# Words of weights fetched a block ahead, and quotients on another engine, in a kernel of hash attention and an MLP mixer

## The chip, the cores and the metric

The kernel runs on one core of a Trainium2 chip. A core has five engines with an instruction queue each, and each works through its queue in order: TensorE (PE in the profile, with its weight loads shown apart as PEld) multiplies matrices, VectorE (DVE) and ScalarE (ACT) work element by element, GpSimd (POOL) does so too, and SyncE (SP) issues transfers. SBUF is the memory in which tiles lie; PSUM holds what TensorE sums up. Engines wait for each other by semaphores. The metric is the device time of one execution in microseconds (us), as the median of several runs; less is better.

## The reference

Two blocks, one behind the other. `q`, `k`, `v` have the shape 4 x 8 x 768 x 64 (batch, head, position, feature).

```python
q_bits = (np.einsum('bhsd,dk->bhsk', q, proj) > 0)        # 6 bits, k likewise
mask = q_bucket[:, :, :, None] == k_bucket[:, :, None, :]  # the same 6 bits
scores = scale * np.matmul(q, k.transpose(0, 1, 3, 2))
scores = np.where(mask, scores, -1000000000.0)
attn = np.exp(scores - np.max(scores, axis=-1, keepdims=True))
attn = attn / (np.sum(attn, axis=-1, keepdims=True) + 1e-09)
x = np.matmul(attn, v)            # heads side by side: 4 x 768 x 512
...
xt = x.transpose(0, 2, 1)
h = np.maximum(xt @ w_tok1, 0.0) @ w_tok2        # over positions
u = x + h.transpose(0, 2, 1)
h2 = np.maximum(u @ w_ch1, 0.0) @ w_ch2          # over channels
return u + h2
```

The four matrices of weights come as 64-bit floats. The kernel reads each as two 32-bit words and rounds it to 32 bits itself.

## The kernel before

It has three stages.

**Attention** (`attention`). The 32 heads are worked on in 16 pairs, a pair in two halves of 384 queries. `Half.scores` multiplies keys by queries for the six groups of 128 keys (L299), each with a second product of hash bits (`bits`) that lowers the scores of other buckets; `exponential` on ScalarE (L306) makes the tiles `e`, of which there are twelve, two halves' worth. `Half.add` adds the six tiles `e` of a half up: GpSimd adds two of them (`esa`, L329), VectorE the others (L331, L332, L334) and then the two sums (L335). `Half.weigh` multiplies `e` by the values `vn` (L345, result `acc`), and ScalarE moves the result to `num` with a bias `vsum` (L351). `Half.weigh` of a half is queued behind the scores of the next half.

Once the two halves of a pair are done, `Quotients` follows in the first half of the next pair: TensorE sums over partitions (`sums`, L369), ScalarE makes a first value of the reciprocal (`near`, L373 and L374), VectorE improves it (`newton`, L382 to L390), and `divide` multiplies `num` by it into `XT` (L394, GpSimd). In the same first half `hashes` makes the bits of the next pair: TensorE (`hp`, L266), VectorE (`g`, L271 and L274), and eight small transfers on SyncE that put them into `bits` (L280). Three tiles of `bits` take turns. `load_qk` and `load_v` fetch queries, keys and values of later pairs; `add_values` (ScalarE, L257) adds the transposed values `vt` up into `vsum`.

**Conversion.** Beside this, `Conversion` rounds the weights in blocks of 128 x 768. A block has three thirds, one in each half from the second pair on, 30 halves in all: `begin` (ScalarE L165, VectorE L167 and L170), `join` (VectorE L182, GpSimd L185 and L186) and `end` (ScalarE L195, VectorE L196). `some` runs them in turn, between the half's additions and its `weigh`. The words of a block lie in the tile `raw`, of which attention has one, and `fetch` (L154, SyncE) asks for the next block's words after `end`. Attention converts eight blocks (`w_tok1`, `w_tok2` and half of `w_ch1`) in 24 of the halves.

**Tokens** (`tokens`). `turn` transposes a batch on TensorE (L226) and ScalarE copies it (L227); `mix1` (L570) and `mix2` (L583) are the two products over positions, and VectorE adds the result to `XT` (L589). A list of jobs, one after each step, rounds the twelve blocks left, with three buffers of `raw`, and forms sums of weights (`weight_sums`, L613 to L618). `inputs` (L540 to L544) forms sums of `XT`.

**Channels** (`channels`). The two products over channels, with 7 block products in place of 8 (L639), and the outputs. Beside them VectorE looks at all queries and keys for their largest value (`look`, `decide`); from it comes a flag `unsafe`. At the very end all engines read the flag (L835) and branch: when it is set, the whole is computed again in a safer way, which these inputs don't ask for.

The order on each engine is the order in which the code calls its operations; nothing rearranges it.

Of the kernel before, what the change touches and what calls it, by code (L numbers as in the profile page):

```python
# [48 lines left out]
def kernel(  # L49
# [13 lines left out]
    nc = tc.nc  # L63
# [62 lines left out]
    class Conversion:  # L126
# [30 lines left out]
        def begin(self):  # L157
            if not self.fetched:
                return
            raw, to, rows = self.fetched.pop(0)  # L160
            lo, hi = raw[:, :, 0], raw[:, :, 1]
            tmp = self.pool.tile([P, 2, NW], F32, name="tmp", tag="cvt", bufs=min(self.bufs, 2))
            big = tmp[:, 0].bitcast(U32)

            nc.scalar.activation(lo.bitcast(F32), lo, ACT.Copy, scale=2.0**-52)  # L165

            nc.vector.tensor_scalar(  # L167
                big, hi, 3, 0x3FFFFFFF, op0=ALU.logical_shift_left, op1=ALU.bitwise_and,
            )
            nc.vector.scalar_tensor_tensor(  # L170
                big, hi, 0xC0000000, big, op0=ALU.bitwise_and, op1=ALU.bitwise_or,
            )
            self.begun = raw, tmp, to, rows
# [27 lines left out]
        def some(self, k):  # L201

            (self.begin, self.join, self.end)[k]()
            if k == 2:
                self.fetch()

        def one(self):
# [20 lines left out]


    def attention(pool, psum, W1, W2, x0):  # L230
        zeroed = [pool.tile([P, 2, S], BF16, name=f"bits{n}", tag=f"bits{n}", bufs=1) for n in range(3)]
        loaded = {}

        def load_qk(n):
# [8 lines left out]
        def load_v(n):  # L243
            if n >= len(pairs):
                return
            b, hp = pairs[n]
            vn = pool.tile([P, 2, NR, D], F32, name="vn", tag="vn", bufs=3)
            nc.sync.dma_start(out=vn, in_=v[b, hp])
            vt = pool.tile([P, S], F32, name="vt", tag="vt", bufs=2)
            nc.sync.dma_start(out=vt, in_=vT[b, hp])  # L250
            loaded[n][1:3] = vn, vt

        def add_values(n):

            vt = loaded[n][2]
            vsum = pool.tile([P, 1], F32, name="vsum", tag="vsum", bufs=4)
            nc.scalar.activation(vt, vt, ACT.Copy, scale=-EPS, accum_out=vsum)  # L257
            loaded[n][3] = vsum

        def hashes(n):  # L260

            g = pool.tile([P, HALF], BF16, name="g", tag="g", bufs=2)
            ps = psum.tile([P, 2, 512], F32, name="hp", tag="sc", bufs=3)[:, 0]
            for j in range(4):
                sl = slice(HALF * (j // 2), HALF * (j // 2) + HALF)
                nc.tensor.matmul(  # L266
                    ps[32 * j : 32 * j + 32, :HALF], projblk, loaded[n][0][:, j % 2, sl],
                    start=True, stop=True,
                )
            for rows in [slice(0, 64), slice(64, P)] if n == 0 else [slice(0, P)]:  # L270
                nc.vector.tensor_scalar(  # L271
                    g[rows], ps[rows, :HALF], 0.0, 0.5, op0=ALU.is_gt, op1=ALU.subtract,
                )
                nc.vector.tensor_scalar(g[rows], g[rows], bitscale[rows], None, op0=ALU.mult)  # L274
            for j in range(4):
                sl = slice(HALF * (j // 2), HALF * (j // 2) + HALF)
                for i in range(2):
                    at = 32 * j + 16 * i
                    issuer = nc.scalar if n == 0 and i else nc.sync
                    issuer.dma_start(  # L280
                        out=zeroed[n % 3][D * i : D * i + NB + 1, j % 2, sl], in_=g[at : at + NB + 1],
                    )

        class Half:
# [4 lines left out]

            def scores(self):  # L290

                qkt, bits = loaded[self.n][0], zeroed[self.n % 3]
                qs = slice(HALF * self.half, HALF * self.half + HALF)
                first = self.n == self.half == 0

                def product(sc, t, c, start):
                    for i in range(2):
                        rows = slice(D * i, D * i + D)
                        nc.tensor.matmul(  # L299
                            sc[:, i, :HALF], t[rows, 1, P * c : P * c + P], t[rows, 0, qs],  # L300
                            start=start, stop=not start,
                        )

                def exponential(sc):
                    e = pool.tile([P, 2, HALF], F32, name="e", tag="e", bufs=12)
                    nc.scalar.activation(e, sc[:, :, :HALF], ACT.Exp, scale=SCALE)  # L306
                    self.es.append(e)

                waiting = []
                for c in range(NR):  # L310
                    sc = psum.tile([P, 2, 512], F32, name="sc", tag="sc", bufs=3)
                    product(sc, qkt, c, True)
                    if first and c < GR:
                        waiting.append((c, sc))
                        if c == GR - 1:
                            for c, sc in waiting:
                                product(sc, bits, c, False)
                            for c, sc in waiting:
                                exponential(sc)
                        continue  # L320
                    product(sc, bits, c, False)
                    exponential(sc)
# [34 lines left out]
        class Quotients:  # L357
# [33 lines left out]

            def divide(self):
                b, hp = pairs[self.n]
                nc.gpsimd.tensor_tensor(  # L394
                    XT[:, hp, S * b : S * b + S].rearrange("p (h q) -> p h q", h=2),
                    nums.pop(self.n), self.rec, op=ALU.mult,
                )
# [9 lines left out]
        for _ in range(14):  # L407
            nc.tensor.matmul(idle[:D, :D], ones, ones, start=True, stop=True)
        hashes(0)
        load_v(0)  # L410
        load_v(1)
        weights = Conversion(
            pool,
            [(w_tok1, W1, 3, (0, NR)), (w_tok2, W2, 1, (0, NJ)), (w_ch1, WC1, 1, (0, NCB // 2))],
            bufs=1,
        )
        before, both = None, []
        third = 0
        for n in range(len(pairs)):
            for half in range(2):  # L420
                now = Half(n, half)
                now.scores()
                if n == half == 0:
                    add_values(0)
                now.add(0)
                quotients = None
                if len(both) == 2:
                    quotients, both = Quotients(both), []
                    quotients.sums()
                both.append(now)  # L430
                if half == 0 and n + 1 < len(pairs):
                    hashes(n + 1)
                    load_qk(n + 2)
                if half == 1 and n + 1 < len(pairs):
                    add_values(n + 1)
                if quotients:
                    quotients.newton()
                now.add(1)
                if n:
                    weights.some(third)  # L440
                    third = (third + 1) % 3
                if before:
                    before.weigh()
                if quotients:
                    quotients.divide()
                if half == 0:
                    load_v(n + 2)
                before = now
        while third or weights.fetched:
            weights.some(third)  # L450
# [171 lines left out]
    def channels(pool, psum, SW1, WC2, SW2, T, judge):  # L622
# [135 lines left out]
        for s in range(last + 1):  # L758
            rs = []
            for t in range(HC):  # L760
                r = pool.tile([P, 4, TT], F32, name="r2", tag="r2", bufs=HC)
                hidden(s, t, r)
                rs.append(r)
                if s or t:
                    look()
                if judge and s == last and t == 1:
                    assert not unseen
                    rest = decide()
                if judge and s == last and t == 4:
                    rest()  # L770
            outputs(s, rs)

    def inside(stage, *args):
# [15 lines left out]
    def attention_and_tokens(W1, W2, x0):  # L789
# [6 lines left out]

        def weights(pool):
            return Conversion(
                pool, [(w_ch1, WC1, 1, (NCB // 2, NCB)), (w_ch2, WC2, 3, (0, NHT))], bufs=3,
            )  # L800

        def jobs(conversion):
            n1, n2 = (NCB // 2) * DCH // NW, NHT * DM // NW
            return [
                *[conversion.one] * (n1 + 1),
                *weight_sums(
# [24 lines left out]
        inside(tokens, W1, W2, x0, None, None, [big["T"][0], None, big["T"][1], None])  # L831

    with_token_weights(attention_and_tokens)
    inside(channels, big["SW1"], big["WC2"], big["SW2"], big["T"], True)
    flag = nc.values_load(unsafe, min_val=0, max_val=1)  # L835
    with tc.If(flag > 0):
        with_token_weights(careful_attention_and_tokens)
        inside(channels, big["SW1"], big["WC2"], big["SW2"], big["T"], False)

# [41 lines left out]
```

## Time and profile before

| | |
|---|---|
| median of 3 runs | 887.88 us (887.83 to 888.03) |
| the profiled execution | 890.64 us |
| its span, first to last instruction | 888.7 us |
| its mean granted TensorE clock | 0.987 |

Busy time of the engines by stage, in the profiled execution (us from the start of the span):

| stage | TensorE | VectorE | ScalarE | GpSimd |
|---|---|---|---|---|
| attention, 0 to 345 | 325.86 | 262.42 | 211.04 | 145.00 |
| tokens, 345 to 450 | 99.79 | 83.24 | 38.37 | 55.84 |
| channels, 450 to 888.7 | 433.05 | 198.01 | 56.17 | 48.73 |

A row of a timeline reads: start and duration in us, engine, line, operation, what it writes and reads, the shape, how many in one, and in brackets how long the engine was idle before it and what ended that. A row of a line's own view gives the shortest, the median and the longest duration in ns and the first and last start. In the chain of work that ended last, a row has start, duration and what the end waited for.

### The profile page before, as it was taken

Reading aid. Unit: us, or ns where it says so; the run is one execution under the profiler, and the core shown is the slowest. Engines: PE = TensorE matmul, PEld = TensorE weight load, DVE = VectorE, ACT = ScalarE, POOL = GpSimd, SP = SyncE. Lnnn points to the kernel's source line nnn. Section 1 sums busy time; section 2 is a strip of 40 time slices with the busy share of each in tenths; the row PEclk is TensorE's granted clock in tenths of the full one; section 3 lists DMA queues with packets and bytes.
Section 4 is the critical chain, followed back from the end, with each engine's and each line's share of the span. In section 5 each row is a group of like instructions: output and inputs, shape, how many; then the busy total and the mean of one; then the engine's idle time right before and its main releaser. Section 6 shows DMA issues by size and latency. Waiting matters only on the chain.

```text
span 888.7 us, 9246 instructions
## 1 busy us (share of the span) xinstructions
PE 858.7 (97%) x3545; PEld 398.6 (45%) x3545; DVE 543.7 (61%) x625; ACT 305.6 (34%) x445; POOL 249.6 (28%) x140
## 2 busy tenths in 40 slices
PE   8998998998999999999899999999999999999997
PEld 4443443443444445455444444444444444444444
DVE  2686986896886777598984475434448342336411
ACT  3765666656656664334312110002120101211000
POOL 3352552553454422556621111201111200111110
PEclk8999999999999999999999999999999999999999
DMA  5223323323332201233211211131220120000001
GB/s 181 98 74 104 117 87 116 131 76 110 109 104 80 73 3 52 92 107 106 71 36 36 72 35 60 35 142 36 71 72 0 60 83 24 1 0 1 24 24 52
DMA packets 20644, 61.16 MB, mean 69 GB/s; under 512 B 2800, under 2 KB 4464, under 8 KB 20592
## 3 DMA queue, kind: packets, MB, share of 16 engines
q1 hardware_dynamic: 20536, 60.46, 20.0%
q8 instruction: 30, 0.49, 0.2%
q14 instruction: 22, 0.18, 0.1%
q10 hardware_dynamic: 56, 0.02, 0.0%
HBM read 53.49 MB, written 6.29 MB: 67 GB/s over the span
## 4 chain that ended last, share of the span: by engine, by line
PE 81%; DVE 10%; DMA 3%; ACT 2%; issue 2%; POOL 1%; SPq 0%; DVEq 0%; ACTq 0%
PE b L639 49%; PE sc L299 13%; PE acc L345 10%; PE t L570 4%; PE t L583 3%; DMA raw<-in_moe_w_tok 2%; DVE esd L335 2%; ACT e L306 1%; PE sums L369 1%; DVE WC L196 1%; DMA raw<-in_moe_w_ch 1%; DVE tmp L170 1%; PE hp L266 1%; PE trp L226 1%; DVE rec L390 1%
## 5 line engine op out<-in xcount | busy, mean ns | idle before, releaser
L299 PE MATMUL sc<-qk 64*128 64x384 f32 x768 | 166.9, 514 | 15.9 <-ACT e L306 15.5
L306 ACT ACTIVATE e<-sc 128x768 f32<-128x768 f32 x192 | 151.5, 811 | 29.8 <-PE sc L299 29.7
L646 ACT COPY p<-b 128x512 f32<-128x512 f32 x72 | 42.1, 585 | 294.2 <-PE b L639 294.2
L345 PE MATMUL acc<-e,vn 128*64 128x384 f32 x768 | 130.9, 490 | 0.0
L639 PE MATMUL b<-r,WC 128*128 128x512 f32 (+1 forms) x300 | 125.6, 575 | 0.0
L299 PEld LDWEIGHTS sc<-qk 64*128 64x128 f32 x768 | 69.4, 195 | 75.9 <-issue 44.9
L639 PE MATMUL b<-T,SW 128*128 128x512 f32 x216 | 96.6, 592 | 0.0
L665 POOL TENSOR_TENSOR p<-p,p 128x512 f32<-128x512 f32 x18 | 22.9, 1271 | 238.9 <-ACT p L646 238.9
L329 POOL TENSOR_TENSOR esa<-e 128x768 f32<-128x768 f32 x32 | 71.0, 2224 | 67.3 <-ACT e L306 67.3
L639 PEld LDWEIGHTS b<-r,WC 128*128 128x128 f32 x300 | 57.0, 190 | 67.1 <-issue 64.1
L345 PEld LDWEIGHTS acc<-e,vn 128*64 128x64 f32 x768 | 52.3, 137 | 74.9 <-issue 74.2
L185 POOL TENSOR_TENSOR tmp<-tmp,raw 128x768 f32<-128x768 f32 x20 | 41.6, 2082 | 100.4 <-DVE tmp L182 63.0
L639 PE MATMUL b<-T,WC 128*128 128x512 f32 x144 | 67.7, 592 | 0.0
L331 DVE TENSOR_TENSOR esd<-e 128x768 f32<-128x768 f32 x32 | 37.1, 1159 | 49.1 <-ACT e L306 49.1
L299 PE MATMUL sc<-bits 64*128 64x384 bf16 x384 | 64.9, 332 | 1.3 <-DMA bits<-g 1.3
L669 DVE TENSOR_TENSOR r<-p,u 128x512 f32<-128x512 f32 x18 | 12.4, 691 | 86.7 <-ACT u L646 86.7
L639 PE MATMUL b<-XT,WC 128*128 128x512 f32 x144 | 64.7, 592 | 0.0
L639 PEld LDWEIGHTS b<-T,SW 128*128 128x128 f32 x216 | 41.0, 190 | 51.7 <-issue 49.7
L639 PE MATMUL b<-r,SW 128*128 128x512 f32 x144 | 62.8, 592 | 0.0
L394 POOL TENSOR_TENSOR XT<-num,rec 128x768 f32<-128x768 f32 x16 | 37.5, 2346 | 77.1 <-ACT num L351 39.7
L335 DVE SCALAR_TENSOR_TENSOR esd<-esd,esa 128x768 f32<-128x768 f32 x32 | 52.8, 1649 | 9.7 <-POOL esa L329 6.8
L186 POOL TENSOR_TENSOR tmp<-tmp 128x768 f32<-128x768 f32 x20 | 46.0, 2302 | 1.6
(84 smaller groups left out, 952.2 us busy)
## 6 DMA issues: line engine op xcount, KB each, us to landing
raw<-in_moe_w_ch SPq DMA_DIRECT2D x16, 768.0 KB
seen<-in_qk SPq DMA_DIRECT2D x16, 768.0 KB
qk<-in_qk SPq DMA_DIRECT2D x15, 768.0 KB
vn<-in_v SPq DMA_DIRECT2D x16, 384.0 KB
vt<-in_vT SPq DMA_DIRECT2D x16, 384.0 KB
out<-p SPq DMA_DIRECT2D x18, 256.0 KB
raw<-in_moe_w_tok SPq DMA_DIRECT2D x4, 768.0 KB
bits<-g SPq DMA_DIRECT2D x124, 5.2 KB
```

The source lines that it names most:

```text
L185: nc.gpsimd.tensor_tensor(unit, unit, lo, op=ALU.mult)
L186: nc.gpsimd.tensor_tensor(big, big, unit, op=ALU.add)
L299: nc.tensor.matmul(sc[:, i, :HALF], t[rows, 1, P * c : P * c + P], t[rows, 0, qs], start=start, stop=not start,)
L306: nc.scalar.activation(e, sc[:, :, :HALF], ACT.Exp, scale=SCALE)
L329: nc.gpsimd.tensor_tensor(self.a, es[0], es[1], op=ALU.add)
L331: nc.vector.tensor_tensor(self.d, es[2], es[3], op=ALU.add)
L335: nc.vector.scalar_tensor_tensor(self.d, self.d, NR * EPS, self.a, op0=ALU.add, op1=ALU.add,)
L345: nc.tensor.matmul(acc[D * i : D * i + D], vn[:, i, c], e[:, i], start=(c == 0), stop=(c == NR - 1),)
L394: nc.gpsimd.tensor_tensor(XT[:, hp, S * b : S * b + S].rearrange("p (h q) -> p h q", h=2), nums.pop(self.n), self.rec, op=ALU.mult,)
L570: nc.tensor.matmul(ps, W1[:, r, P * j : P * j + P], x[:, r], start=(r == 0), stop=(r == NR - 1),)
L639: nc.tensor.matmul(self.ps[i][:, cols], left(k), right(k)[:, cols], start=first and k == ks[0], stop=k == ks[-1], skip_group_check=True,)
L646: nc.scalar.copy(c, self.ps[i])
```

## The change

Five edits go together.

- In attention `raw` gets a second buffer, and `fetch` follows `begin` in place of `end`, so a block's words are asked for when the block before begins.
- `divide` runs on VectorE.
- Attention converts two more blocks (three of the four rows of `w_ch1`, ten blocks, 30 halves); the tokens stage has two fewer, and two jobs fewer.
- For room in SBUF there are two tiles of `bits` and of `vn` in place of three; values are loaded one pair ahead in place of two, and `add_values` of a pair runs in its own first half, not in the second half of the pair before.
- The flag is read ahead of the last `outputs`.

```diff
-            tmp = self.pool.tile([P, 2, NW], F32, name="tmp", tag="cvt", bufs=min(self.bufs, 2))
+            tmp = self.pool.tile([P, 2, NW], F32, name="tmp", tag="cvt", bufs=self.bufs - 1)
...
             (self.begin, self.join, self.end)[k]()
-            if k == 2:
+            if k == 0:
                 self.fetch()
...
-        zeroed = [pool.tile([P, 2, S], BF16, name=f"bits{n}", tag=f"bits{n}", bufs=1) for n in range(3)]
+        zeroed = [pool.tile([P, 2, S], BF16, name=f"bits{n}", tag=f"bits{n}", bufs=1) for n in range(2)]
...
-            vn = pool.tile([P, 2, NR, D], F32, name="vn", tag="vn", bufs=3)
+            vn = pool.tile([P, 2, NR, D], F32, name="vn", tag="vn", bufs=2)
...
                 b, hp = pairs[self.n]
-                nc.gpsimd.tensor_tensor(
+                nc.vector.tensor_tensor(
                     XT[:, hp, S * b : S * b + S].rearrange("p (h q) -> p h q", h=2),
...
         load_v(0)
-        load_v(1)
         weights = Conversion(
             pool,
-            [(w_tok1, W1, 3, (0, NR)), (w_tok2, W2, 1, (0, NJ)), (w_ch1, WC1, 1, (0, NCB // 2))],
-            bufs=1,
+            [(w_tok1, W1, 3, (0, NR)), (w_tok2, W2, 1, (0, NJ)), (w_ch1, WC1, 1, (0, NCB - 1))],
+            bufs=2,
         )
...
-                if n == half == 0:
-                    add_values(0)
+                if half == 0:
+                    add_values(n)
...
-                if half == 1 and n + 1 < len(pairs):
-                    add_values(n + 1)
...
                 if half == 0:
-                    load_v(n + 2)
+                    load_v(n + 1)
...
+            if judge and s == last:
+                flags.append(nc.values_load(unsafe, min_val=0, max_val=1))
             outputs(s, rs)
...
-                pool, [(w_ch1, WC1, 1, (NCB // 2, NCB)), (w_ch2, WC2, 3, (0, NHT))], bufs=3,
+                pool, [(w_ch1, WC1, 1, (NCB - 1, NCB)), (w_ch2, WC2, 3, (0, NHT))], bufs=3,
...
-            n1, n2 = (NCB // 2) * DCH // NW, NHT * DM // NW
+            n1, n2 = DCH // NW, NHT * DM // NW
...
+    flags = []
     inside(channels, big["SW1"], big["WC2"], big["SW2"], big["T"], True)
-    flag = nc.values_load(unsafe, min_val=0, max_val=1)
-    with tc.If(flag > 0):
+    with tc.If(flags[0] > 0):
```

On VectorE the quotient (L394) now stands at the end of each pair's first half. Here is that place in the third pair to convert, behind the additions and L182 of the first half and ahead of the additions of the second:

```order
 L335 SCALAR_TENSOR_TENSOR esd<-esd,esa 128x768
 L182 TENSOR_SCALAR tmp<-tmp 128x768
+L394 TENSOR_TENSOR XT<-num,rec 128x768
 L331 TENSOR_TENSOR esd<-e 128x768
 L332 TENSOR_TENSOR esd<-esd,e 128x768
```

Nothing else moved on VectorE in a half; one operation came in.

On GpSimd the same place before, from the conversion of the block (L185, L186) to the additions of the second half and of the next pair's first half:

```order
L185 TENSOR_TENSOR tmp<-tmp,raw 128x768
L186 TENSOR_TENSOR tmp<-tmp 128x768
L394 TENSOR_TENSOR XT<-num,rec 128x768
L329 TENSOR_TENSOR esa<-e 128x768 x2
L394 TENSOR_TENSOR XT<-num,rec 128x768
```

and with the change:

```order
L185 TENSOR_TENSOR tmp<-tmp,raw 128x768
L186 TENSOR_TENSOR tmp<-tmp 128x768
L329 TENSOR_TENSOR esa<-e 128x768 x3
L185 TENSOR_TENSOR tmp<-tmp,raw 128x768
L186 TENSOR_TENSOR tmp<-tmp 128x768
```

The quotients are gone from GpSimd, and each block's two operations are followed by the additions of three halves.

On SyncE, from the first transfer of words to the second one (between them `bits`, queries and keys, values of the next pairs), before:

```order
L154 DMA raw<-in_moe_w_tok 128x3x512
L280 DMA bits_105<-g 7x384 x8
L240 DMA qk<-in_qk 128x1536
L248 DMA vn<-in_v 128x768
L250 DMA vt<-in_vT 128x768
L280 DMA bits_106<-g 7x384 x8
L240 DMA qk<-in_qk 128x1536
L248 DMA vn<-in_v 128x768
L250 DMA vt<-in_vT 128x768
L280 DMA bits_104<-g 7x384 x8
L240 DMA qk<-in_qk 128x1536
L154 DMA raw<-in_moe_w_tok 128x3x512
```

and with the change:

```order
L154 DMA raw<-in_moe_w_tok 128x3x512
L280 DMA bits_105<-g 7x384 x8
L240 DMA qk<-in_qk 128x1536
L248 DMA vn<-in_v 128x768
L250 DMA vt<-in_vT 128x768
L280 DMA bits_104<-g 7x384 x8
L240 DMA qk<-in_qk 128x1536
L154 DMA raw<-in_moe_w_tok 128x3x512
```

The second block's words stood behind the third group of `bits`, in the third pair; now they stand behind the second, in the second pair. So it goes on: the words of each block are asked for two halves earlier.

More of the change, by code (lines that the diff above doesn't have):

```diff
@@ L280, in hashes @@
                     issuer.dma_start(
-                        out=zeroed[n % 3][D * i : D * i + NB + 1, j % 2, sl], in_=g[at : at + NB + 1],
+                        out=zeroed[n % 2][D * i : D * i + NB + 1, j % 2, sl], in_=g[at : at + NB + 1],
                     )
@@ L290, in scores @@
             def scores(self):
-                qkt, bits = loaded[self.n][0], zeroed[self.n % 3]
+                qkt, bits = loaded[self.n][0], zeroed[self.n % 2]
                 qs = slice(HALF * self.half, HALF * self.half + HALF)
```

## The prediction

> **What bounds the kernel now.** I read the busy shares first, then the chain of work that ended last in order of time, then the list of waits, then the timelines of VectorE, GpSimd and TensorE in the stretches where the chain leaves TensorE.
>
> ```profile
> span 888.7 us, 9246 instructions
> ...
> PE 858.7 (97%) x3545; PEld 398.6 (45%) x3545; DVE 543.7 (61%) x625; ACT 305.6 (34%) x445; POOL 249.6 (28%) x140
> ```
>
> From the list of waits (who for whom: us in total, times, longest):
>
> ```profile
> ACT raw L165 <- DMA raw<-in_moe_w_ch: 24.9, 5, 6.6
> ...
> ACT raw L165 <- DMA raw<-in_moe_w_tok: 17.0, 3, 6.6
> ...
> PE sc L299 <- ACT e L306: 15.5, 5, 3.8
> ...
> PEld sums L369 <- DVE esd L335: 1.5, 4, 0.4
> ```
>
> TensorE is busy for 858.7 of 888.7 us, so only what makes it wait or run slowly is to be had. Its largest wait is 15.5 us in five pieces for the exponentials of ScalarE, and ScalarE itself sat 24.9 + 17.0 us in L165 until words of weights had landed. The chain (start, us, what) shows how the two hang together:
>
> ```profile
> 112.87 2.64 PE sc L299 x18
> ...
> 194.03 2.51 DVE WC L196
> 196.59 4.53 DMA raw<-in_moe_w_ch
> ...
> 202.03 0.57 ACT num L351
> ...
> 203.35 4.26 PE sc L299 x18
> ```
>
> With one `raw` buffer the next words are asked for only when L196 has read the last (196.54); they land 4.53 us later; L165 stands in ScalarE's queue ahead of `num` and of the next exponentials, so TensorE waits. Behind the wait 18 score matmuls take 4.26 us where they take 2.64 elsewhere: another 1.6 us.
>
> What all of this costs in attention follows from the pace of `hp`, the hash product that stands once in each pair of heads:
>
> ```profile
> 34.00 0.65 PE hp L266 x8
> ...
> 143.58 0.65 PE hp L266 x8
> ...
> 163.66 0.65 PE hp L266 x7
> ...
> 293.31 0.65 PE hp L266 x7
> 312.87 0.65 PE hp L266 x8
> ```
>
> An undisturbed pair takes 312.87 - 293.31 = **19.56 us**. From 34.00 to 312.87 there are 13 pairs: 278.87 us, against 13 x 19.56 = 254.3. The excess is **24.6 us**. One kind of it is the DMA stall, four times (the fifth piece of TensorE's wait lies at the start of the kernel), and the other is short: 143.58 to 163.66 is 20.08, 0.5 too long, four times as well, so the stalls are (24.6 - 2.1) / 4 = 5.6 us each. The 0.5 comes from VectorE and GpSimd:
>
> ```profile
> 169.55 2.51 POOL L394 TENSOR_TENSOR XT<-num,rec 128x768 f32<-128x768 f32 x1 [7.60 <-DVE rec L390]
> ```
>
> ```profile
> 160.22 2.55 DVE L335 SCALAR_TENSOR_TENSOR esd<-esd,esa 128x768 f32<-128x768 f32 x1 [1.70 <-POOL esa L329]
> ...
> 170.50 2.38 DVE L335 SCALAR_TENSOR_TENSOR esd<-esd,esa 128x768 f32<-128x768 f32 x1
> ...
> 175.90 0.96 DVE L331 TENSOR_TENSOR esd<-e 128x768 f32<-128x768 f32 x1
> ...
> 179.97 0.55 DVE L182 TENSOR_SCALAR tmp<-tmp 128x768 uint32<-128x768 uint32 x1
> ```
>
> An addition takes 0.96 us alone (175.90) and 2.38 (170.50) when a GpSimd operation is under way; it ends 0.82 us after that operation (172.88 and 172.06), so the two take turns. At 160.22 L335 also waited 1.70 us for GpSimd's L329, which had stood behind L185, L186 and L394 in its queue; `sums` on TensorE then waited for L335, as the list of waits has it four times.
>
> **The change, part by part.** *Words a block ahead.* The fetch moves from a block's last third to its first, into a second buffer. A block's words are then asked for three halves of a pair (3 x 9.78 = 29 us) before L165 reads them, against 4.53 us to land. Of the 5.6 us stalls nothing is left as long as the order of SyncE lets the transfer start. There it stands behind the eight `bits` transfers and `qk`, ahead of or behind `vn` and `vt` of the next pair, and waits only for the L196 of an earlier half. Removed: **24.6 us**, the short ones included, since what replaces those is counted next.
>
> *What is late next.* The same work of VectorE and GpSimd now has to fit into pairs of 19.56 us, with conversion in all 30 halves, ten blocks where there were eight. I add it up for three pairs (58.7 us, two blocks).
>
> ```profile
> 209.11 0.56 DVE L271 TENSOR_SCALAR g<-hp 128x384 bf16<-128x384 f32 x1 [0.46 <-PE hp L266]
> ...
> 213.04 0.96 DVE L334 TENSOR_TENSOR esd<-esd,e 128x768 f32<-128x768 f32 x1
> ```
>
> By line (ns of the shortest, the median and the longest):
>
> ```profile
> L331 DVE TENSOR_TENSOR esd<-e x32: 941/960/2575, 15.5 to 340.8; 128x768 f32<-128x768 f32 x32
> ```
>
> ```profile
> L167 DVE TENSOR_SCALAR tmp<-raw x20: 544/562/2191, 42.0 to 439.9; 128x768 uint32<-128x768 uint32 x20
> ```
>
> ```profile
> L382 DVE TENSOR_TENSOR t<-sums,near x16: 542/550/558, 35.5 to 350.4; 128x384 f32<-128x384 f32 x16
> ```
>
> ```profile
> L329 POOL TENSOR_TENSOR esa<-e x32: 1802/2520/2547, 13.4 to 339.3; 128x768 f32<-128x768 f32 x32
> ```
>
> ```profile
> L394 POOL TENSOR_TENSOR XT<-num,rec x16: 1814/2512/2531, 39.4 to 353.8; 128x768 f32<-128x768 f32 x16
> ```
>
> VectorE: the four additions of a half take 4.07 us from start to start (175.90 to 179.97), six times, 24.4; bits and reciprocals 3.93 (209.11 to 213.04), three times, 11.8; a block L167 0.56, L182 0.55, and L170 and L196, of the shape of L331, 0.96 each, together 3.03, twice, 6.1. New is the quotient: the trace has none on VectorE, and the nearest row is L331, of the same shape with two inputs in SBUF, from 0.94 us alone to 2.58 when it takes turns with GpSimd. I take 0.96, since the turn is GpSimd's time and is counted there: three times, 2.9. VectorE: 45.2 us. GpSimd, undisturbed: L329 1.80 six times, 10.8; L185 and L186, of that kind too, 1.8 each, two blocks, 7.2. Its 3 x 1.81 of L394 go. GpSimd: 18.0. Of VectorE's operations L382, which reads PSUM, is never stretched (558 ns at most), and I take L271, which reads it too, likewise: 0.55 us each, 3.3 in three pairs.
>
> So 45.2 + 18.0 - 3.3 = 59.9 us take turns in 58.7: **1.2 us too much in three pairs**. (Before, with L394 on GpSimd, the same sum is 62.4.) It shows where 0.5 was lost before: `sums` waits for the second half's L335 of the pair whose first half starts GpSimd's conversion. Five times three pairs: **+6.0 us**; bounds 0, where the engines' turns fall well, and 15, where 3 us are lost each time.
>
> On those turns the Trainium skill's page "SBUF — State Buffer" (section "Who interferes with whom") says that a VectorE operation with two SBUF inputs and a GpSimd operation that reads SBUF lock each other out. The rows above agree; by a rule without a lock VectorE's 45.2 us alone would count, and the 6.0 would be 0.
>
> *Edits that I cost at nothing.* L257 moves from the second half to the first, ahead of `near`: 0.84 us, about 1 with the read of its sum. `near` is read by L382, 1 us later then; ScalarE has to be done only when `num` is due, and was idle 2.71 us ahead of it with L195 done:
>
> ```profile
> L257 ACT ACTIVATE vt<-vt x16: 833/835/836, 18.6 to 323.3; 128x768 f32<-128x768 f32 x16
> ```
>
> ```profile
> 177.44 0.58 ACT L351 ACTIVATE num<-acc,vsum 128x384 f32<-128x384 f32 x1 [2.40 <-PE acc L345]
> ...
> 187.94 0.58 ACT L351 ACTIVATE num<-acc,vsum 128x384 f32<-128x384 f32 x1 [2.71 <-PE acc L345]
> ```
>
> Were that cover gone, 16 x 1.0 us would be the price. The buffers of `bits`, `vn` and `vt` that go were not waited for: with two, each is free once the pair before has been read. `vt` is now loaded in the pair ahead of its use, about 15 us into it, behind `qk`, `vn` and in each third pair a block of words; all four one after the other, at 4.53 us for 768 KB, take 13.6 us and land 9 us into the next pair, 3 us behind L257's place. That uses up the 2.71 us and no more; a microsecond in five pairs, 5 us, is the most I can make of it.
>
> The flag: five engines load it, and the rows of two show when.
>
> ```profile
> L835 SPq TENSOR_LOAD <-unsafe x1: 477/477/477, 801.2 to 801.2; - x1
> ...
> L835 PEldq TENSOR_LOAD <-unsafe x1: 532/532/532, 879.0 to 879.0; - x1
> ```
>
> ```profile
> L836 SPq EVENT_SEMAPHORE  x8: 17/17/17, 884.6 to 887.3; - x8
> ```
>
> SyncE loaded it at 801.2 already, and the end waits for the last output (887.3), so nothing is won there. Moved, TensorE's load stands between matmuls; its sequencer ran some 4 us ahead (it loaded at 879.0, and the outputs that end at 887.3 hang on the last matmul), which covers 0.53 us. I take 0, with -0.5 and +0.5 as ends.
>
> *Tokens stage.* Two blocks fewer leave 10 to convert there.
>
> ```profile
> 432.34 5.43 PE L583 MATMUL t<-W,r 128*128 128x384 f32 x16 [1.64 <-DVE XT L589]
> 438.62 5.43 PE L583 MATMUL t<-W,r 128*128 128x384 f32 x16 [0.85 <-DVE XT L589]
> 444.88 5.43 PE L583 MATMUL t<-W,r 128*128 128x384 f32 x16 [0.84 <-DVE XT L589]
> ```
>
> ```profile
> L613 DVE TENSOR_TENSOR SW<-WC x2: 1746/1746/1747, 390.0 to 450.8; 128x1536 f32<-128x1536 f32 x2
> ```
>
> The first of these waits lies behind L540, L541 and two whole jobs, which stay: it stays. Ahead of the second and third stood a whole job each; now only an L196 and a pair of L613's kind (3.5 us), which fit beside 5.43 us of matmuls. **-1.7 us**, at least 0 and at most 3.3.
>
> **The sum.** -24.6 + 6.0 - 1.7 = -20.3 us. The profiled execution took 890.64 us (its span 888.7), the median of the runs is 887.88; 2.8 us less; the sum gives 870.3 with a profile, and from 887.88 **867.6 us** without.
>
> **Rivals.** *No lag:* the lock's turns fall into VectorE's idle time and `sums` never waits. For it: VectorE's own 45.2 of 58.7. Against: the 0.5 us waits before, in stretches that started on time. 887.9 - 24.6 - 1.7 = **861.6**.
>
> *The move of the quotients does not pay.* If a quotient costs VectorE as much turn as it took from GpSimd, the excess in three pairs is 62.4 - 58.7 = 3.7 us, five times 18.5: 887.9 - 24.6 - 1.7 + 18.5 = **880.1**. For it: L331's 2.58 us at the longest. Against: 0.96 us beside 1.81. The Trainium skill's page "Perfetto Trace Analysis" (section "Optimizing Scalar/DVE Operations") warns that moving work between these two might not help, for their common port.
>
> *The words still come late,* because SyncE holds them behind a wait: one stall of 5.6 us in each three pairs, five now: 887.9 - 24.6 + 28 - 1.7 = **889.6**. Against: the words have 29 us.
>
> *Slower:* VectorE's lag reaches `g`. The bits of a pair are sent by eight transfers, and the next pair's scores need them.
>
> ```profile
> 166.42 5.90 SPq L280 DMA_DIRECT2D bits<-g  x8
> ```
>
> ```profile
> 9.00 1.83 DMA bits<-g
> ```
>
> Sent from 166.42 they had landed by 166.42 + 5.90 + 1.83 = 174.2, and the scores began when `num` did, 177.4: 3.2 us to spare. For a slower kernel more than the sum's 26.3 us must come back, 1.75 in each of 15 pairs: `g` would have to be 3.2 + 1.75 = 5 us later than here, in every pair, where the count above finds 1.2 in three. Past that it is slower; with 2 us a pair 887.9 - 26.3 + 30 = **892**.
>
> **How the numbers follow.** Forecast (865 to 872) 0.48, no lag (860 to 865) 0.24, quotients that do not pay (872 to 881) 0.20, words still late 0.03, slower 0.05. Range 860.5 to 877, which leaves out the last two cases and the end of the third. By 0.2% (1.8 us, what a measurement can tell from no change) or more faster: 0.92; within: 0.03; slower: 0.05.
>
> **What would show it.** Right: no wait of L165 for `raw` in attention, `hp` every 19.6 us but for about 1.2 us more each third pair, ahead of `sums` and released by `esd`; no full-length L394 on GpSimd; two of the three waits at L589 gone; the end as before. Wrong: a wait of `sc` on `bits`, L165 still waiting for `raw`, or pairs that are all longer than 20 us.

## The result and the profile after

| | before | changed |
|---|---|---|
| median | 887.95 us (887.83 to 891.85, 4 runs) | 863.22 us (862.52 to 866.67, 4 runs) |
| ratio to before, 95% interval | | 0.9719 (0.9682 to 0.9756) |
| the profiled execution | 890.64 us | 862.8 us |
| its span | 888.7 us | 860.9 us |

The kernel is 24.7 us faster. In the changed kernel the lines of the tokens and channels stages carry numbers that are three lower: L583 is now L580, L589 is L586, L639 is L636.

From the page of the changed kernel, its span and busy time:

```profile
span 860.9 us, 9280 instructions
...
PE 847.9 (98%) x3545; PEld 395.2 (46%) x3545; DVE 558.2 (65%) x641; ACT 304.7 (35%) x445; POOL 214.2 (25%) x123
```

From its list of waits (who for whom: us in total, times, longest):

```profile
ACT raw L165 <- DMA raw<-in_moe_w_ch: 2.8, 1, 2.8
...
PEld sums L369 <- DVE esd L335: 1.0, 1, 1.0
...
PE sc L299 <- ACT e L306: 0.7, 1, 0.7
```

No wait for words is left in attention; the 2.8 us lie in the tokens stage, where 11.7 of the 41.9 us lay before. TensorE's 15.5 us for exponentials have become 0.7. The chain shows what that does to the pace:

```profile
31.80 0.65 PE hp L266 x8
...
51.36 0.65 PE hp L266 x8
...
266.53 0.65 PE hp L266 x8
...
286.09 0.65 PE hp L266 x8
```

13 pairs take 286.09 - 31.80 = 254.29 us, 19.56 each; before they took 278.87. All **24.6 us** of excess are gone, and nothing has come in their place. The timeline of TensorE behind the last pair has the two waits that remain of those the prediction spoke of:

```profile
322.61 0.85 PE L369 MATMUL sums<-esd,ones 128*32 128x384 f32 x6 [0.34 <-DVE esd L335]
...
407.62 15.75 PE L580 MATMUL t<-W,r 128*128 128x384 f32 x48 [2.52 <-DVE XT L586]
423.20 3.60 PE L636 MATMUL b<-XT,WC 128*128 128x512 f32 x8
```

In the tokens stage three waits for `XT` (3.33 us) have become one of 2.52. Yet from the last `hp` to the first product of the channels stage it is 423.20 - 286.09 = 137.11 us, and it was 450.15 - 312.87 = 137.28: what the tokens stage won, the end of attention lost.

The two spans differ by 27.8 us: 24.6 in the pairs, 0.2 from there to the channels stage, 0.9 behind the channels' start, and 2.2 ahead of the third pair. Those 2.2 belong to the execution that was profiled of the kernel before: its granted TensorE clock was 0.90 in the first 34 us, where the changed kernel's was 1.00, and it lay 2.8 us above the median. The medians differ by 24.7, about the first two terms.

So the lag of 1.2 us in three pairs that the prediction expected did not show. VectorE of the changed kernel, from a half with `end` to the second half of the next pair (idle time and its cause in brackets):

```profile
225.89 1.22 DVE L331 TENSOR_TENSOR esd<-e 128x768 f32<-128x768 f32 x1 [1.52 <-ACT e L306]
...
255.94 2.36 DVE L331 TENSOR_TENSOR esd<-e 128x768 f32<-128x768 f32 x1 [0.16 <-ACT e L306]
258.41 2.38 DVE L332 TENSOR_TENSOR esd<-esd,e 128x768 f32<-128x768 f32 x1
260.90 2.38 DVE L334 TENSOR_TENSOR esd<-esd,e 128x768 f32<-128x768 f32 x1
263.38 0.96 DVE L335 SCALAR_TENSOR_TENSOR esd<-esd,esa 128x768 f32<-128x768 f32 x1
```

and the `sums` that wait for that L335 of 263.38:

```profile
265.68 0.85 PE L369 MATMUL sums<-esd,ones 128*32 128x384 f32 x8
```

L335 ends at 264.34 and `sums` begins at 265.68: 1.3 us to spare. The place is the predicted one, but the lag stays short of it. How full the three pairs are is the question of the experiments.

### The profile page after: what moved, and what is told of

Read it like the earlier page. It is cut to its first block, busy times and chain, and to the rows that moved or that the text cites. A ratio compares the mean times of both kernels' runs of the same rounds, so it can differ in the third digit from the quotient of the medians.

```text
span 860.9 us, 9280 instructions
## 1 busy us (share of the span) xinstructions
PE 847.9 (98%) x3545; PEld 395.2 (46%) x3545; DVE 558.2 (65%) x641; ACT 304.7 (35%) x445; POOL 214.2 (25%) x123
## 4 chain that ended last, share of the span: by engine, by line
PE 91%; DVE 5%; DMA 1%; ACT 1%; issue 1%; SPq 0%; DVEq 0%; ACTq 0%
PE b L636 50%; PE sc L299 18%; PE acc L345 14%; PE t L580 3%; PE t L567 3%; PE hp L266 1%; PE sums L369 1%; DVE tmp L170 1%; DVE WC L196 1%; DVE tmp L167 1%; DMA raw<-in_moe_w_ch 1%; DMA qk<-in_qk 0%; DVE esd L334 0%; PE trp L226 0%; DVE T L537 0%
## 5 line engine op out<-in xcount | busy, mean ns | idle before, releaser
L299 PE MATMUL sc<-qk 64*128 64x384 f32 x768 | 159.5, 495 | 0.7 <-ACT e L306 0.7
L636 PE MATMUL b<-r,WC 128*128 128x512 f32 (+1 forms) x300 | 125.6, 575 | 0.0
L329 POOL TENSOR_TENSOR esa<-e 128x768 f32<-128x768 f32 x32 | 73.0, 2282 | 117.8 <-ACT e L306 101.9
L636 PE MATMUL b<-T,SW 128*128 128x512 f32 x216 | 96.6, 592 | 0.0
L299 PEld LDWEIGHTS sc<-qk 64*128 64x128 f32 x768 | 67.2, 188 | 56.9 <-issue 46.9
L636 PEld LDWEIGHTS b<-r,WC 128*128 128x128 f32 x300 | 57.0, 190 | 67.1 <-issue 64.1
L185 POOL TENSOR_TENSOR tmp<-tmp,raw 128x768 f32<-128x768 f32 x20 | 43.7, 2183 | 124.8 <-DVE tmp L182 79.1
L666 DVE TENSOR_TENSOR r<-p,u 128x512 f32<-128x512 f32 x18 | 12.5, 693 | 91.4 <-ACT u L643 91.4
L636 PE MATMUL b<-T,WC 128*128 128x512 f32 x144 | 67.7, 592 | 0.0
L636 PEld LDWEIGHTS b<-T,SW 128*128 128x128 f32 x216 | 41.0, 190 | 51.7 <-issue 51.7
L636 PE MATMUL b<-XT,WC 128*128 128x512 f32 x144 | 64.7, 592 | 0.0
L636 PE MATMUL b<-r,SW 128*128 128x512 f32 x144 | 62.8, 592 | 0.0
L331 DVE TENSOR_TENSOR esd<-e 128x768 f32<-128x768 f32 x32 | 40.8, 1275 | 19.9 <-ACT e L306 19.9
L332 DVE TENSOR_TENSOR esd<-esd,e 128x768 f32<-128x768 f32 x32 | 45.1, 1408 | 3.3
L351 ACT ACTIVATE num<-acc,vsum 128x384 f32<-128x384 f32 x32 | 18.6, 580 | 80.3 <-PE acc L345 80.3
L186 POOL TENSOR_TENSOR tmp<-tmp 128x768 f32<-128x768 f32 x20 | 45.1, 2257 | 1.6
```

The lines of the kernel that those rows point to most:

```text
L185: nc.gpsimd.tensor_tensor(unit, unit, lo, op=ALU.mult)
L186: nc.gpsimd.tensor_tensor(big, big, unit, op=ALU.add)
L299: nc.tensor.matmul(sc[:, i, :HALF], t[rows, 1, P * c : P * c + P], t[rows, 0, qs], start=start, stop=not start,)
L329: nc.gpsimd.tensor_tensor(self.a, es[0], es[1], op=ALU.add)
L331: nc.vector.tensor_tensor(self.d, es[2], es[3], op=ALU.add)
L332: nc.vector.tensor_tensor(self.d, self.d, es[4], op=ALU.add)
```

## The experiments

Each was compared with the kernel before, on the same chip. Unless something else is said, a kernel is the changed one with one edit.

**One buffer** (`one_buffer`): the prefetch undone, the rest kept (`tmp` keeps its one buffer).

```diff
-            if k == 0:
+            if k == 2:
                 self.fetch()
...
-            bufs=2,
+            bufs=1,
```

> The changed kernel with one buffer of words again and the fetch after a block's last third; all other edits stay. If the late words made the gain, stalls of about 5.6 us come back, five of them now (ten blocks): 863 + 28 = 891 us, at least 863 + 22.6 = 886. If the relief of GpSimd made most of it, the last third ends earlier, the words too, and the time stays below 875.

Measured 891.14 us, ratio 1.0024 (1.0009 to 1.0039). In its list of waits:

```profile
ACT raw L165 <- DMA raw<-in_moe_w_ch: 29.5, 7, 8.0
...
PE sc L299 <- ACT e L306: 18.0, 6, 4.3
```

All of the gain is gone: the other four edits together gain nothing without the prefetch. Of the ten waits of ScalarE for words, eight lie in attention and two in the tokens stage (before: five and three). TensorE loses time once in three pairs, as before: such a pair takes 25.3 to 26.4 us, where it took 24.9 to 25.2.

**Asked for at the end** (`fetch_at_end`): two buffers, but the fetch after `end`.

```diff
-            if k == 0:
+            if k == 2:
                 self.fetch()
```

> The changed kernel with two buffers, but the fetch after a block's last third. If the second buffer alone is enough (the transfer no longer waits for L196), 863 to 865 us. If the words must also be asked for earlier: where the last third lies in a pair's first half, the transfer starts about 16 us into the pair and L165 of the next block wants it at about 16.5, so L165 waits some 4.5 us, of which 3 are free until num is due; 1.5 to 3 us of stall in each three pairs, 871 to 878 us.

Measured 881.19 us, ratio 0.9900 (0.9872 to 0.9928), slower than either expectation: three pairs lose 2.4 to 6.2 us, where 1.5 to 3 were expected. Its chain shows one of the stalls that are left:

```profile
187.55 0.44 SPq L240
188.11 6.75 DMA raw<-in_moe_w_ch
195.03 0.67 issue
195.70 0.57 ACT num L351
196.26 0.71 ACT e L306
197.02 5.17 PE sc L299 x18
```

With two buffers SyncE is free to ask before L196, but where `end` falls in a pair's first half the words stand in its queue behind the eight `bits` transfers and `qk`, and 6.75 us to land are too long from there. From `one_buffer` to this kernel the second buffer brings 10.0 us; asking two halves earlier brings the other 18.0.

**Quotients on GpSimd** (`q_gpsimd`), and the **fetch alone** (`fetch_alone`: second buffer and early fetch with the edits that make room; quotients, eight blocks and flag as before).

```diff
-                nc.vector.tensor_tensor(
+                nc.gpsimd.tensor_tensor(
                     XT[:, hp, S * b : S * b + S].rearrange("p (h q) -> p h q", h=2),
```

> The changed kernel with the quotients on GpSimd again. Theory A (the count of the prediction: turns add up in full, 62.4 us of work in 58.7): 3.7 us more in each three pairs, 880 us. Theory B (a GpSimd operation adds only what it stretches VectorE's by, 2.38 - 0.96 = 1.42 us: 42.3 + 13 x 1.42 - 3.3 = 57.5 us, which fits into 58.7): at most 0.5 us in each three pairs, 863 to 866 us.

> Only the second buffer, the early fetch and the edits that make room for it; quotients on GpSimd, eight blocks in attention, the flag at the end, as before. By theory A 62.4 us of work in 58.7 for four times three pairs: 863 + 15 = 878 us. By theory B the fetch is nearly the whole gain: 862 to 866 us.

Measured: `q_gpsimd` 874.63 us, ratio 0.9855 (0.9830 to 0.9879); `fetch_alone` 873.29 us, 0.9832 (0.9815 to 0.9848). Both lie between the two theories, nearer A: with the quotients on GpSimd a lag does appear. GpSimd and VectorE of `q_gpsimd` in one of the pairs concerned:

```profile
78.83 1.85 POOL L185 TENSOR_TENSOR tmp<-tmp,raw 128x768 f32<-128x768 f32 x1 [9.77 <-DVE tmp L182]
80.76 2.41 POOL L186 TENSOR_TENSOR tmp<-tmp 128x768 f32<-128x768 f32 x1
83.13 2.52 POOL L394 TENSOR_TENSOR XT<-num,rec 128x768 f32<-128x768 f32 x1
85.61 4.30 POOL L329 TENSOR_TENSOR esa<-e 128x768 f32<-128x768 f32 x2
```

```profile
84.09 2.38 DVE L334 TENSOR_TENSOR esd<-esd,e 128x768 f32<-128x768 f32 x1
88.17 2.56 DVE L335 SCALAR_TENSOR_TENSOR esd<-esd,esa 128x768 f32<-128x768 f32 x1 [1.70 <-POOL esa L329]
```

L394 holds L329 up by 2.5 us, L335 waits 1.70 us for it, and `sums` waits for L335. In TensorE's timeline of `q_gpsimd`:

```profile
90.78 0.52 PE L369 MATMUL sums<-esd,ones 128*32 128x384 f32 x3 [1.10 <-DVE esd L335]
...
274.52 0.52 PE L369 MATMUL sums<-esd,ones 128*32 128x384 f32 x3 [1.31 <-DVE esd L335]
```

Nine pairs take 274.52 - 90.78 = 183.74 us, 61.25 for three, against 58.68: **2.6 us too much in three pairs**. The quotients' move is worth 874.63 - 863.22 = 11.4 us once the words come in time. While they come late, it and the three smaller edits gain nothing together (`one_buffer`); the move alone was not tried there.

**One and two extra additions** (`extra1`, `extra2`): ahead of each quotient VectorE makes one or two more sums of 128x768, which nothing reads.

```diff
+                for _ in range(1):
+                    spare = pool.tile([P, 2, HALF], F32, name="spare", tag="spare", bufs=1)
+                    nc.vector.tensor_tensor(spare, self.halves[0].d, self.halves[1].d, op=ALU.add)
```

(`range(2)` in the second.)

> The changed kernel with one more addition of 128x768 on VectorE ahead of each quotient (its result is not used). Theory A: 59.9 + 2.9 = 62.8 us of work in 58.7 in three pairs, some 4 us more each, 880 us. Theory B: 56.1 + 2.9 = 59.0 us, 0.3 too much in three pairs: 863 to 866 us; by the 3.1 us that VectorE is idle in three pairs of the changed kernel it just fits.

> The same with two more additions ahead of each quotient. Theory A: 65.7 us in 58.7, 7 us in each three pairs, about 898 us. Theory B: 56.1 + 5.8 = 61.9 us, 3.2 too much in each three pairs, about 879 us; TensorE then waits for sums (esd) or for bits.

Measured: `extra1` 876.22 us, ratio 0.9845 (0.9821 to 0.9868); `extra2` 892.04 us, ratio 1.0028 (1.0013 to 1.0043). Both lie between the theories, nearer A. The waits of `sums` in `extra1`, the first and the last one before the end of attention:

```profile
91.24 0.52 PE L369 MATMUL sums<-esd,ones 128*32 128x384 f32 x3 [1.14 <-DVE esd L335]
...
275.85 0.52 PE L369 MATMUL sums<-esd,ones 128*32 128x384 f32 x3 [1.38 <-DVE esd L335]
```

Three pairs take 184.61 / 3 = 61.54 us, 2.86 more for 3 x 0.96 = 2.88 added. In `extra2` they take 64.43 as the mean of nine pairs (63.8, 64.4 and 65.1 one by one), 5.75 more for 5.76. Added in every pair, a microsecond costs one: on this mean the three pairs of the changed kernel are **full**, although VectorE idles 1.5 us of it in one piece, ahead of the half with `end` that is the first of its pair. GpSimd uses that time; in the changed kernel it has

```profile
224.45 1.84 POOL L185 TENSOR_TENSOR tmp<-tmp,raw 128x768 f32<-128x768 f32 x1 [6.89 <-DVE tmp L182]
```

while VectorE idles from 224.4 to 225.9.

**Two extra additions in one pair of three** (`extra2_first` in the pair with `begin` in its first half, `extra2_third` in the one with `join`).

```diff
+                for _ in range(2 if self.n % 3 == 0 else 0):
```

(`== 2` in the second.)

> This kernel is the changed one with two additions of 128x768, whose result nothing reads, on VectorE ahead of the quotient, but only in every third pair: the one in whose first half the conversion is at `begin` (five pairs). Stretch theory: only the stretch from L331 in the first half of the pair with `end` to L335 of the second half of the next pair is tight; the pair chosen here lies outside it, and its additions (5 x 1.92 us) fall into VectorE's idle time ahead of the stretch (1.5 us in each three pairs): 863 to 865 us. Average theory: VectorE and GpSimd fill 58.7 us of three pairs whatever the place, 1.92 us more per three pairs cost what two thirds of the fifteen quotients of the kernel with one extra addition cost: 13.0 x 2/3 = 8.7 us, so 870 to 873 us.

> The same two unread additions, but in the pairs in whose first half the conversion is at `join` (five pairs, among them the last but one that converts). Stretch theory: these stand inside the tight stretch, which has 1.4 us to spare: at least 1.92 - 1.4 = 0.5 us, and up to 2 us where a turn with GpSimd is added, in each of five places: 866 to 873 us, with waits of `sums` for L335 of 0.5 to 2 us each. Average theory: as for the other place, 870 to 873 us; the two kernels are then equal within 1 us.

Measured: `extra2_first` 869.78 us, ratio 0.9775 (0.9751 to 0.9799); `extra2_third` 875.16 us, ratio 0.9839 (0.9812 to 0.9867). Neither theory holds as it was put. The place counts, 5.4 us of it, against the average theory; but `extra2_first`, at 869.8, is no free ride either, against the stretch theory. Three pairs take 59.98 and 60.81 us: the 1.92 us that were added cost 1.30 in the one place and 2.13 in the other, so "full" is a statement about the mean and not about each place. VectorE of `extra2_first` in the stretch that follows, the rows that answer to those from 255.94 above:

```profile
200.85 2.61 DVE L331 TENSOR_TENSOR esd<-e 128x768 f32<-128x768 f32 x1
203.56 2.38 DVE L332 TENSOR_TENSOR esd<-esd,e 128x768 f32<-128x768 f32 x1
206.05 2.38 DVE L334 TENSOR_TENSOR esd<-esd,e 128x768 f32<-128x768 f32 x1
208.54 2.38 DVE L335 SCALAR_TENSOR_TENSOR esd<-esd,esa 128x768 f32<-128x768 f32 x1
```

Measured from `hp` of their pairs (190.94 here, 246.97 there), L331 starts 9.91 us behind `hp` in place of 8.97: half of the 1.92 us was taken up by idle time, 0.94 is left, which the 1.3 us to spare ahead of `sums` would have held. But L335 now falls into a turn with the next L329 of GpSimd and takes 2.38 where it took 0.96. That makes it 17.60 + 2.38 against 16.41 + 0.96, 2.6 us late, of which 1.3 were to spare, and `sums` waits. What an addition costs depends on which VectorE operations it pushes into GpSimd's turns.

In `extra2_third` the additions stand beside GpSimd's conversion and are stretched themselves:

```profile
200.10 3.47 DVE L396 TENSOR_TENSOR spare<-esd 128x768 f32<-128x768 f32 x2
203.49 2.57 DVE L397 TENSOR_TENSOR XT<-num,rec 128x768 f32<-128x768 f32 x1
205.99 2.55 DVE L331 TENSOR_TENSOR esd<-e 128x768 f32<-128x768 f32 x1
```

**Eight blocks** (`eight_blocks`: eight blocks in attention, twelve in the tokens stage, whose list of jobs is as before) and the **flag last** (`flag_last`).

```diff
-            [(w_tok1, W1, 3, (0, NR)), (w_tok2, W2, 1, (0, NJ)), (w_ch1, WC1, 1, (0, NCB - 1))],
+            [(w_tok1, W1, 3, (0, NR)), (w_tok2, W2, 1, (0, NJ)), (w_ch1, WC1, 1, (0, NCB // 2))],
```

```diff
-            if judge and s == last:
-                flags.append(nc.values_load(unsafe, min_val=0, max_val=1))
             outputs(s, rs)
...
+    flag = nc.values_load(unsafe, min_val=0, max_val=1)
+    with tc.If(flag > 0):
```

> The changed kernel with eight blocks in attention and twelve in tokens, as before. The wait for sums at the end of attention (0.34 us in the trace, some 1 us with what is late beside it) goes, and the waits for L589 in tokens come back (3.33 in place of 2.52): 862.5 to 864 us, no difference that can be measured. If two blocks more in attention are worth the 1.7 us of the prediction: 865 us.

> The changed kernel with the flag read at the very end again. The prediction put the edit at 0: 863.2 us. The stretch behind the last matmul was 0.8 us shorter in the changed kernel's trace (860.9 - 856.1 = 4.8 against 888.7 - 883.1 = 5.6); if the flag did that: 864.0 us.

Measured: `eight_blocks` 862.79 us, ratio 0.9697 (0.9678 to 0.9716); `flag_last` 864.41 us, ratio 0.9715 (0.9695 to 0.9734). Neither edit makes a difference that these times separate. With eight blocks the three waits of the tokens stage are back, and the end of attention has none:

```profile
321.24 0.85 PE L369 MATMUL sums<-esd,ones 128*32 128x384 f32 x8
...
405.40 5.43 PE L580 MATMUL t<-W,r 128*128 128x384 f32 x16 [1.66 <-DVE XT L586]
411.67 5.43 PE L580 MATMUL t<-W,r 128*128 128x384 f32 x16 [0.84 <-DVE XT L586]
417.94 5.43 PE L580 MATMUL t<-W,r 128*128 128x384 f32 x16 [0.84 <-DVE XT L586]
423.20 3.60 PE L636 MATMUL b<-XT,WC 128*128 128x512 f32 x8
```

The channels stage begins at 423.20 in both. With the flag last it ends 5.6 us after the last matmul (855.93 to 861.5), as before, and 4.8 with the flag early (856.10 to 860.9). The other traces agree: in all eleven with the flag early this end takes 4.6 to 5.3 us, in the three with it last 5.5 to 5.6. So the early flag shortens the end by some 0.7 us; the medians, which differ by 1.2 with intervals that overlap, are too coarse to show it.

**Inputs later** (`inputs_later`), and **both later** (`both_later`: besides, the second job of each `mix1` but the last stands behind the next `turn`).

```diff
-            if b == 2:
+            if b == 3:
                 inputs(0, T, 0)
```

```diff
                 turn(b, x, banks)
+                job()
...
-                job()
+                if j == 0 or b == B - 1:
+                    job()
```

> The changed kernel with the first half of `inputs` (L537, L538) asked for one batch later in the tokens stage, so that L537 and L538 no longer stand ahead of L586 on VectorE at the one wait of 2.52 us that is left there. Theory that this wait is only the queue ahead of L586: the wait goes, 863.2 - 2.5 = 860.7 us. Rival: the wait moves to the next batch, or the channels stage begins late for T: 863 us or more.

> As the kernel before this one, and the second job of each `mix1` but the last runs after the `turn` of the next batch, so that ScalarE's L165 or L195 stand behind its L227 and not ahead of it. The profile of the changed kernel has TensorE waiting 1.42, 0.24 and 0.23 us for L227 there: expected 860.7 - 1.4 to 1.9 = 859 us. Rival: the job then comes late for L586 or for the weights of the channels stage, and the gain is given back: 861 us or more.

Measured: `inputs_later` 862.18 us, ratio 0.9698 (0.9677 to 0.9720), which its interval does not separate from the changed kernel; `both_later` 867.88 us, ratio 0.9763 (0.9742 to 0.9784), 5.7 us slower than `inputs_later`. TensorE's two last waits in `inputs_later`, and in `both_later`:

```profile
404.22 10.59 PE L580 MATMUL t<-W,r 128*128 128x384 f32 x32 [0.15 <-DVE XT L586]
416.49 5.43 PE L580 MATMUL t<-W,r 128*128 128x384 f32 x16 [1.69 <-DVE XT L586]
```

```profile
409.07 12.06 PE L582 MATMUL t<-W,r 128*128 128x384 f32 x32 [5.00 <-DVE XT L588]
422.81 5.43 PE L582 MATMUL t<-W,r 128*128 128x384 f32 x16 [1.69 <-DVE XT L588]
```

In the first, the wait of 2.52 us goes and 1.69 of it returns one batch later, where `inputs` now stands, as its rival had it. In the second the 1.42 us for L227 are gone (0.23 left), but the postponed jobs pile up: VectorE rounds four blocks one behind the other, from 386.0 to 408.5, before it comes to L588. The rival was right there. No run is faster than the changed kernel by more than the intervals allow.

## Why the prediction was right, and where its size was off

The prediction's 867.6 us lay 4.4 above what was measured; 863.2 is inside its range, but below the forecast's own 865 to 872, in the band that it gave to the rival *no lag*.

- *Words a block ahead, -24.6 us.* Right in mechanism and size: 24.6 us gone from the 13 pairs, no wait of L165 for `raw` in attention. `one_buffer` gives all of the gain back; `fetch_at_end` shows that the buffer without the earlier request would not have done.
- *What is late next, +6.0 us.* **This is the term that was mis-sized: 0 in the pairs.** Mechanism and place were right: VectorE and GpSimd take turns, and where their work is too much, `sums` waits for the L335 that was named, as in `q_gpsimd`, `fetch_alone` and `extra1`. The count of turns was 59.9 us for three pairs. Less what was added, `extra1` and `extra2` put it at 58.7, just what the pairs hold, and the two runs with additions in one pair of three at 58.1 and 58.9. With the quotients on GpSimd the count was 62.4, an excess of 3.7; measured 2.6. So it was 1 to 2 us too high, 2 to 3%, and its difference, 2.5 for the move of the quotients, came out at 2.6. An excess of 1.2 us is no larger than that error. Which price was too high isn't settled. My guess is the 1.80 us for each of ten GpSimd operations: a VectorE addition that waits for one takes 2.38 in place of 0.96, 1.42 more. But ten times 1.42 would leave 2.6 us to spare, which `extra1` excludes; 1.68 would fit the mean. `extra2_first` shows why no single price holds: it depends on what the operations fall beside.
- *No lag* had the time but not the reason. It let the turns fall into idle time without cost, with VectorE's 45.2 us of 58.7 in its favour. Then 13.5 us in three pairs would have been free for more work; `extra1` pays 13.0 us in the whole kernel for 15 x 0.96 = 14.4 us of additions.
- *The move of the quotients does not pay* is refuted: `q_gpsimd` is 11.4 us slower. By the prediction's own count the move saved 18.5 - 6.0 = 12.5. The warning of the Trainium skill's page "Perfetto Trace Analysis" (section "Optimizing Scalar/DVE Operations"), that work moved between these two engines might not help, does not hold here: a quotient costs 0.95 us on VectorE and 1.8 to 2.5 on GpSimd. The exclusive lock of the Trainium skill's page "SBUF — State Buffer" (section "Who interferes with whom") agrees with `extra1` and `extra2` in that added time costs its full length; turns of 0.96 and 1.80 us in full, as the prediction counted them, are too many.
- *Tokens, -1.7 us.* Half right: two of the three waits went, but the first grew from 1.64 to 2.52. L537 and L538 take as long as before (2.86 and 2.85 us, against 2.85 and 2.84), but VectorE comes to L537 3.93 us after TensorE began the last `turn` products (392.46 and 388.53), where it was 3.06 (417.20 and 414.14); why it comes later was not tried. And the conversion that now goes on to the last half of attention costs 1.2 us there, which the prediction left out: from the last `hp` to the end of the last wait of `sums` it is 322.61 - 286.09 = 36.52 us, with eight blocks 321.24 - 285.90 = 35.34. Net about 0.2; `eight_blocks` comes out equal.
- *Edits at nothing.* L257 cost nothing: all pairs take 19.56 us. The flag costs nothing either and shortens the end by some 0.7 us, a little beyond the 0.5 that the prediction gave as the most. The prediction read only SyncE's and TensorE's load of the flag; VectorE's, in the trace before, starts at 883.1, with the last matmul's end. The slower rival never came near.

## What to carry to other kernels

When a stall goes, the load that it covered becomes the bound: here moving the quotients was worth 11 us once the stall was gone, while under the stall the move and three smaller edits gained nothing together; the fetch alone was worth 16 of 25. Whether two engines that take turns still have room is not read from idle time; add known work to one of them, in more than one place, and see how much of its length it costs. And a second buffer helps only in part, here by 10 of 28 us, if the request still stands late in its queue.

## What the runs showed of the hardware

- An addition of 128x768 on VectorE that meets an operation of GpSimd goes from 0.96 to 2.38 us, the GpSimd one from 1.8 to about 2.5. Small copies in SBUF are stretched too: in `extra2_first` four copies L390 of 32x384 take 2.97 us together where they take 1.45.

```profile
177.86 2.97 DVE L390 COPY rec<-rec 32x384 f32<-32x384 f32 x4
```

- The words landed 4.5 us after the request in the kernel before, and 6.6 to 6.8 us after it in `one_buffer`, though both ask behind L196. In `one_buffer` SyncE had issued `qk`, as large a transfer, 1.2 us earlier, before 3.0 us; that the two share the DMA engines is the likely reason, and was not tried by itself.
- Behind a stall TensorE is slower for a while, but not always: in `fetch_at_end` 18 score matmuls took 5.17 us behind a wait of 3.08 us (197.02 above) and 2.69 behind one of 2.16 (134.98), against 2.64 undisturbed. The granted clock goes with it: 0.50 from 197.0 to 202.2, and 1.00 from 134.9 to 137.7. In the kernel before it was 0.63 from 203.3 to 207.7, where the prediction saw 4.26 us in place of 2.64; so part of each stall's 5.6 us is this lower clock.
